# The left key tiles of a unit's two pairs as four 128x64 column tiles in a row

## The chip, the cores and the metric

The kernel runs on one core of one Trainium2 chip. The metric is device microseconds (us) for one execution of the whole program: 609.46 us before the change, the median of three runs (609.01 to 609.54).

Of the core's engines five matter: TensorE (PE; its weight loads are listed as PEld), ScalarE (ACT), VectorE (DVE), GpSimd (POOL) and SyncE (SP), which issues most of the transfers. TensorE writes into PSUM, eight banks of 128 partitions x 512 fp32 values.

## The reference

Attention with normed q and k over 8 batches, 12 heads, 448 tokens and head size 64, and behind it an MLP with a residual over the 768 columns that the heads make together:

```python
q_n, k_n = (rmsnorm(q, g_q), rmsnorm(k, g_k))
scores = 1.0 / np.sqrt(q.shape[-1]) * np.matmul(q_n, k_n.transpose(0, 1, 3, 2))
attn = np.exp(scores - np.max(scores, axis=-1, keepdims=True))
attn = attn / (np.sum(attn, axis=-1, keepdims=True) + 1e-09)
x = np.matmul(attn, v)              # then (batch, 448, 12 * 64)
xn = (x - mu) / np.sqrt(var + 1e-06) * g_ln
out = x + np.maximum(xn @ w_ch1, 0.0) @ w_ch2        # 768 -> 3072 -> 768
```

## The kernel before

**Pairs and units.** Two heads make a pair; a batch has six pairs, so there are 48, numbered through. Pairs are prepared in units (`UNITS`): units 0 and 1 have one pair, units 2 to 24 two. `PAIR_UNIT[p]` gives a pair's unit and its place in it (0 or 1), `UNIT_PAIR[u]` a unit's first pair. From unit 2 on the first pair of a unit is even and the second odd. Units 5 to 24 hold pairs 8 to 47.

**Scores.** A pair's 448 keys per head are six full tiles of 128 keys (three for each head, steps i = 0 to 5) and a rest of 64 keys per head. The two rests form step 6, the left keys. `scores(p, i)` takes a PSUM bank, lets TensorE write 128 keys x 448 queries of scores there, and ScalarE's `Exp` (L357) takes them as fp16 into `E[:, i]`. The contraction is 128 deep: q and k stand as a high and a low fp16 half. The left keys lie in SBUF as 64 columns of head 0, 64 columns of zeros, 64 columns of head 1. Step 6 takes columns 0 to 127 against head 0's queries (L354) and columns 64 to 191 against head 1's (L355), and sums both in one bank: where one writes scores, the other adds zeros. Both stream 448 columns.

**Score banks.** The pool `ps_s` has two banks. After pair 14 (`UNIT_PAIR[DMA_UNIT]`) the bank `tr`, which until then holds transposes, takes every third score, so three banks rotate.

**Values.** `values(p, i)` multiplies `E[:, i]` as weights with v (L389 and L391) into the banks oA and oB; after step 6 `evac_o` divides by the row sums on VectorE. Step 6 of the values takes the left tile of E and `vl`, 130 columns.

**E.** The pool `p_e` has two buffers of seven tiles; pairs alternate between them.

**Order.** Pairs 0 to 6 come in an order written out by hand (`ORDER`). From there `attention()` lists steps, seven a pair: step (p, i) holds pieces of the preparation of coming units, `scores(p, i)`, `values(p - 1, i)`, the statistics for the norm, and, up to pair 13, transposes of the next pair's k (at i = 2) and q (at i = 4) on TensorE with VectorE's copies. From unit 8 on k and q are transposed by DMA from SP (`dma_k`, `dma_q`, L257 to L270). `run_rest` deals these steps out between the chunks of the MLP of the batch before: a chunk is six matmuls of `up` (L631, psH) or `down` (L647, psC). The last 13 chunks of a batch hold no steps, and there the norm of the next batch runs. TensorE, ScalarE, GpSimd and SP take their instructions in the order written; VectorE's order in this part is set by a scheduler. The k and q buffers (`kU`, `qU`) are two each, by unit.

**The flag.** Once, in the last batch, `flag()` sums a check with a matmul of one weight column (L760).

Of the kernel before, what the change touches and what calls it, by code (L numbers as in the profile page):

```python
# [8 lines left out]
FP32 = mybir.dt.float32  # L9
FP16 = mybir.dt.float16  # L10
# [38 lines left out]
EARLY = {5: (42, 49), 6: (47, 56), 7: (61, 69), 8: (75, 83), 9: (89, 97)}  # L49
LN_EXP_SET = 6  # L50
UP_FIRST = 3
REC_LO, REC_HI = 1.0 / 3.0e7, 0.5
K_MAX = 6.0e4
XS = 32.0
# [21 lines left out]
class _Fast:  # L76


    def __init__(self, ctx, tc, sh, q, k, v, gs, g_ln, w1, w2, out):
        self.gs, self.g_ln = gs, g_ln  # L80
        self.tc, self.nc, self.sh = tc, tc.nc, sh
        self.q, self.k, self.v, self.w1, self.w2, self.out = q, k, v, w1, w2, out
        nc = tc.nc
        pool = lambda name, bufs, **kw: ctx.enter_context(tc.tile_pool(name=name, bufs=bufs, **kw))
        self.p_in = pool("p_in", 2)
        self.p_n = pool("p_n", 2)
        self.p_e = pool("p_e", 2)
        self.p_x = pool("p_x", 2)
        self.p_xl = pool("p_xl", 2)
        self.p_m = pool("p_m", 1)  # L90
        self.fix = pool("fix", 1)
        self.ps_tr = pool("ps_tr", 1, space=PSUM)
        self.ps_s = pool("ps_s", 2, space=PSUM)
        self.ps_o = pool("ps_o", 1, space=PSUM)
        self.ps_m = pool("ps_m", 3, space=PSUM)
        fix = self.fix
        self.kU = [fix.tile([128, 1920], FP16, name=f"kU{i}", tag=f"kU{i}") for i in range(2)]
        self.qU = [fix.tile([128, 2, 2, S], FP16, name=f"qU{i}", tag=f"qU{i}") for i in range(2)]
        self.v16 = fix.tile([128, 6, 2, 3, D + 1], FP16, name="v16", tag="v16")
        self.vl = fix.tile([128, 6, 2, D + 1], FP16, name="vl", tag="vl")  # L100
        nc.vector.memset(self.v16[:, :, :, :, D], 1.0)
        nc.vector.memset(self.vl, 0.0)
        nc.vector.memset(self.vl[0:64, :, 0, D], 1.0)
        nc.vector.memset(self.vl[64:128, :, 1, D], 1.0)
        self.rec = fix.tile([128, B * NPAIR, 4, 2], FP32, name="rec_all", tag="rec_all")
        nc.vector.memset(self.rec, 0.01)
        self.rr = fix.tile([128, len(UNITS)], FP32, name="rr_all", tag="rr_all")
        self.rs = fix.tile([128, B, 4], FP32, name="rs_all", tag="rs_all")
        nc.vector.memset(self.rs, RS_LO)
        self.hT = fix.tile([128, NFF, 512], FP16, name="hT", tag="hT")  # L110
        self.tr = self.ps_tr.tile([128, 1024], FP16, name="tr", tag="tr")
        nc.vector.memset(self.tr[:, 64:128].bitcast(FP32), 0.0)
        self.zero_left(DMA_UNIT)
        self.xs, self.xls, self.st = {}, {}, {}
        self.units, self.loads, self.prs = {}, {}, {}
        self.late, self.preps = [], {}

    def zero_left(self, u):

# [218 lines left out]
    def scores(self, p, i):  # L338

        nc = self.nc  # L340
        c = self.prs[p]
        q, left = c["q"], c["left"]
        if i == 0:
            c["E"] = self.p_e.tile([128, 7, S], FP16, tag="E", name="E")
        if p > UNIT_PAIR[DMA_UNIT] and (7 * p + i) % 3 == 2:
            ps = self.ps_tr.tile([128, 512], FP32, tag="tr", name="psS3")
        else:
            ps = self.ps_s.tile([128, 512], FP32, tag="psS", name="psS")
        if i < 6:
            h = i // 3  # L350
            nc.tensor.matmul(ps[:, 0:S], c["main"][:, ts(i, 128)], q[:, ts(h, S)],  # L351
                             start=True, stop=True)
        else:
            nc.tensor.matmul(ps[:, 0:S], left[:, 0:128], q[:, 0:S], start=True, stop=False)  # L354
            nc.tensor.matmul(ps[:, 0:S], left[:, 64:192], q[:, S:2 * S], start=False, stop=True)  # L355
        g = self.group(p, i)
        nc.scalar.activation(out=c["E"][:, i], in_=ps[:, 0:S], func=AFT.Exp,  # L357
                             scale=self.units[PAIR_UNIT[p][0]][3][:, g:g + 1], bias=EXP_BIAS)

        u = PAIR_UNIT[p][0]  # L360
        if i == 6 and UNIT_PAIR[u] == p and u > 4:
            self.least(u)

    def least(self, u):

# [3 lines left out]
    def values(self, p, i):  # L369
        nc = self.nc  # L370
        c = self.prs[p]
        E = c["E"]
        if i == 0:
            if p in (1, 3, 5):
                c["oA"] = self.ps_m.tile([128, 3, 130], FP32, tag="mlp", name="oA")
                c["oB"] = self.ps_m.tile([128, 130], FP32, tag="mlp", name="oB")
            else:
                c["oA"] = self.ps_o.tile([128, 3, 130], FP32, tag="oA", name="oA")
                c["oB"] = self.ps_o.tile([128, 130], FP32, tag="oB", name="oB")
        oA, oB = c["oA"], c["oB"]  # L380
        if i < 6:
            h, j = divmod(i, 3)
            rhs = self.v16[:, p % 6, h, j]
            cs = slice(65 * h, 65 * h + 65)
        else:
            rhs = self.vl[:, p % 6].rearrange("p e d -> p (e d)")
            cs = slice(0, 130)
        for t in range(3):
            nc.tensor.matmul(oA[:, t, cs], E[:, i, ts(t, 128)], rhs,  # L389
                             start=(i == 0 and t == 0), stop=(i == 6 and t == 2))  # L390
        nc.tensor.matmul(oB[:, cs], E[:, i, 320:448], rhs, start=(i == 0), stop=(i == 6))  # L391
        if i == 6:
            self.evac_o(p)

# [73 lines left out]
    def attention(self):  # L468

        n, nu, nb0, done = B * NPAIR, len(UNITS), NPAIR, set(ORDER)  # L470
        todo, last = {}, -9
        for u in range(4, nu):
            p, m = UNIT_PAIR[u], UNITS[u][2]
            st = max(7 * (p - 2 - m) + 2, last + 1, 7 * nb0)
            e = max(7 * (p - 2) - 1, st + 5)
            st, e = EARLY.get(u, (st, e))
            pieces = ["bai", "d", "c", "e", "j", "gv", "k", "l", "m", "w", "x", "y"]
            k = len(pieces) - 2
            if u < DMA_UNIT:
                pieces = pieces[:k]  # L480
            if f"z{u}" in done and u == 4:
                continue
            if u < nu - 2 and f"L{u + 2}" not in done:
                todo.setdefault(e + (8 if u == DMA_UNIT else 1), []).append(
                    lambda u=u: self.load_unit(u + 2))
            last = e
            for x, names in enumerate(pieces):
                at = st + (e - st) * x // (k - 1) if x < k else e + 1 + x - k
                todo.setdefault(at, []).extend(
                    self.prep_ops(u)[y] for y in names  # L490
                    if not {y + str(u), f"z{u}" if y in "vw" else ""} & done)
                if u in (6, 7) and x == 0:
                    todo[at].append(lambda u=u: self.load_w2(u - 6))
        steps, mark = [], [0]

        for p in range(nb0, n + 1):
            for i in range(7):
                c = []
                if i == 0 and p < n and p % NPAIR == 0 and p > nb0:
                    c.append(lambda b=p // NPAIR: self.batch(b))  # L500
                c += todo.pop(7 * p + i, [])
                if p < n and f"S{p}.{i}" not in done:
                    c.append(lambda p=p, i=i: self.scores(p, i))
                if p > nb0:
                    for x in {0: (), 1: (0, 1)}.get(i, (i,)):
                        if f"V{p - 1}.{x}" not in done:
                            c.append(lambda p=p, x=x: self.values(p - 1, x))
                if p > nb0 + 1 and i == 1 and (p - 1) % NPAIR:
                    c.append(lambda p=p: self.stats(p - 2))
                if p + 1 < UNIT_PAIR[DMA_UNIT]:  # L510
                    if i == 2 and f"K{p + 1}" not in done:
                        c.append(lambda p=p: self.trans_k(p + 1))
                    if i == 4 and f"Q{p + 1}" not in done:
                        c.append(lambda p=p: self.trans_q(p + 1))
                if p > nb0 and p % NPAIR == 0 and i == 6:
                    c.append(lambda p=p: self.stats(p - 1))
                if c:
                    steps.append(c)
            if p > nb0 and p % NPAIR == 0:
                mark.append(len(steps))  # L520
        return steps, mark
# [425 lines left out]
```

## Time and profile before

| What | Value |
|---|---|
| median of three runs | 609.46 us |
| span of the profiled execution | 606.9 us |
| that execution's own time | not listed apart; the median is 2.5 us above the span |
| TensorE busy | 579.4 us, 95% |
| TensorE weight loads busy | 346.4 us, 57% |
| ScalarE busy | 359.5 us, 59% |
| VectorE busy | 287.1 us, 47% |
| GpSimd busy | 190.1 us, 31% |
| left scores L354 and L355 | 48 matmuls each, 17.2 and 17.1 us busy |
| exponentials L357 | 336, 635 ns each on average |
| TensorE waiting for an exponential before a full score | 5.3 us, 14 times |
| granted TensorE clock | 0.996 |

A row of the chain or of the timeline gives the start in us from the span's start, the time in us, the engine, the line of the kernel, the operation, what it writes and reads, shapes, and how many were merged; in brackets stands the idle time before it and what ended it. Matmuls are pipelined: a record of a 448-column matmul lasts 0.35 us, but the next starts 0.19 us after it. ScalarE's records overlap in the same way. In the chain each piece has only the time that it adds.

### The profile page before, as it was taken

Reading aid. Unit: us, or ns where it says so; the run is one execution under the profiler, and the core shown is the slowest. Engines: PE = TensorE matmul, PEld = TensorE weight load, DVE = VectorE, ACT = ScalarE, POOL = GpSimd, SP = SyncE. Lnnn points to the kernel's source line nnn. Section 1 sums busy time; section 2 is a strip of 40 time slices with the busy share of each in tenths; the row PEclk is TensorE's granted clock in tenths of the full one; section 3 lists DMA queues with packets and bytes.
Section 4 is the critical chain, followed back from the end, with each engine's and each line's share of the span. In section 5 each row is a group of like instructions: output and inputs, shape, how many; then the busy total and the mean of one; then the engine's idle time right before and its main releaser. Section 6 shows DMA issues by size and latency. Waiting matters only on the chain.

```text
span 606.9 us, 11525 instructions
## 1 busy us (share of the span) xinstructions
PE 579.4 (95%) x4500; PEld 346.4 (57%) x4500; DVE 287.1 (47%) x643; ACT 359.5 (59%) x673; POOL 190.1 (31%) x245
## 2 busy tenths in 40 slices
PE   2887999999999999999999999999999999999995
PEld 1555666655566666655566666655566666654564
DVE  5799567734256256715256255633356322530011
ACT  5996887268743697458753598538754377124200
POOL 3854432233541355332552345423412000000000
PEclk9899999999999999999999999999999999999999
DMA  8999999478954596747955485748733330030011
GB/s 225 275 192 200 214 225 187 103 211 83 149 157 107 89 136 154 174 133 90 126 129 127 114 123 141 188 120 124 125 74 68 92 62 1 31 100 0 1 53 57
DMA packets 130861, 75.29 MB, mean 124 GB/s; under 512 B 96656, under 2 KB 121040, under 8 KB 130800
## 3 DMA queue, kind: packets, MB, share of 16 engines
q1 hardware_dynamic: 114048, 45.12, 38.3%
q0 software_dynamic: 16080, 28.94, 22.1%
q8 instruction: 37, 0.61, 0.5%
q10 hardware_dynamic: 672, 0.43, 0.2%
q14 instruction: 24, 0.20, 0.1%
HBM read 52.36 MB, written 11.01 MB: 104 GB/s over the span
## 4 chain that ended last, share of the span: by engine, by line
PE 90%; DVE 2%; ACT 0%; issue 0%; DVEq 0%
PE psC L647 36%; PE psH L631 35%; PE psS L351 8%; PE oA L389 5%; PE oB L391 2%; PE psS L354 1%; PE psS L355 1%; PE tr L329 0%; PE tr L315 0%; PE psU L677 0%; DVE stat L555 0%; DVE xn L576 0%; DVE x L406 0%; DVE qU L334 0%; ACT E L357 0%
## 5 line engine op out<-in xcount | busy, mean ns | idle before, releaser
L631 PE MATMUL psH<-xnT,w 128*128 128x512 f16 (+1 forms) x1134 | 241.9, 353 | 0.0
L357 ACT ACTIVATE E<-psS,rr_all 128x448 f16<-128x448 f32 x336 | 207.6, 635 | 49.5 <-PE psS L351 44.3
L647 PE MATMUL psC<-w,hT 128*128 128x384 f16 (+1 forms) x1368 | 234.7, 323 | 0.0
L633 ACT ACTIVATE hT<-psH 128x512 f16<-128x512 f32 (+1 forms) x189 | 104.1, 551 | 124.3 <-PE psH L631 122.3
L647 PEld LDWEIGHTS <-hT 128*128 128x128 f16 x1368 | 127.8, 98 | 74.4
L631 PEld LDWEIGHTS <-w 128*128 128x128 f16 x1134 | 102.6, 98 | 80.5
L351 PE MATMUL psS<-qU,kU 128*128 128x448 f16 x288 | 100.9, 358 | 8.0 <-ACT E L357 5.3
L389 PEld LDWEIGHTS <-E 128*128 128x128 f16 x1008 | 71.2, 99 | 48.7 <-issue 4.1
L228 POOL TENSOR_TENSOR qkv<-qkv,gprod 128x896 f32<-128x896 f32 x21 | 43.7, 2080 | 95.3 <-issue 49.5
L389 PE MATMUL oA<-v,E 128*128 128x65 f16 x864 | 67.0, 194 | 0.1
L651 DVE SCALAR_TENSOR_TENSOR x<-psC,rs_all,x 128x384 f32<-128x384 f32 x48 | 28.9, 615 | 72.0 <-PE psC L647 71.5
L404 DVE RECIPROCAL rec_all<-oA 128x6 f32<-128x6 f32 x48 | 9.3, 193 | 94.0 <-PE oA L389 93.8
L391 PE MATMUL oB<-v,E 128*128 128x65 f16 x288 | 52.0, 194 | 0.1
L127 POOL DMA_DIRECT2D qkv<-in_k_dram x14 | 11.2, 799 | 129.8 <-ACT E L357 60.3
L217 DVE TENSOR_REDUCE ssq<-khl 128x14 f32<-128x896 f32 (+1 forms) x24 | 25.6, 1065 | 44.6 <-ACT khl L214 44.5
L351 PEld LDWEIGHTS <-kU 128*128 128x128 f16 x288 | 28.2, 99 | 25.8 <-issue 6.1
L217 DVE TENSOR_REDUCE ssq<-qn 128x14 f32<-128x896 f32 (+1 forms) x25 | 26.1, 1046 | 21.9 <-ACT qn L214 21.8
L67 DVE SCALAR_TENSOR_TENSOR qn<-qkv,rr_all 128x256 f16<-128x256 f32 (+1 forms) x72 | 26.3, 424 | 15.3 <-ACT rr_all L221 15.3
L391 PEld LDWEIGHTS <-E 128*128 128x128 f16 x336 | 32.7, 97 | 0.3 <-DVE xl L411 0.2
L239 DVE TENSOR_TENSOR khl<-qkv,khl 128x896 f16<-128x896 f32 x21 | 22.7, 1083 | 10.6 <-ACT khl L236 9.7
L406 DVE TENSOR_TENSOR x<-oA,rec_all 128x384 f32<-128x384 f32 x48 | 26.8, 558 | 1.5
L555 DVE BATCH_NORM_STATS2 stat<-x 128x6 f32<-128x256 f32 (+1 forms) x75 | 26.2, 404 | 0.6
(104 smaller groups left out, 448.4 us busy)
## 6 DMA issues: line engine op xcount, KB each, us to landing
out_dram<-x SPq DMA_DIRECT2D x20, 384.0 KB, 2.5
qkv<-in_k_dram POOLq DMA_DIRECT2D x14, 384.0 KB, 3.9
qkv<-in_q_dram POOLq DMA_DIRECT2D x14, 384.0 KB, 5.2
qkv<-in_v_dram POOLq DMA_DIRECT2D x14, 384.0 KB, 7.8
w<-in_moe_w_ch_dram POOLq DMA_DIRECT2D x3, 1536.0 KB, 12.6
w<-in_moe_w_ch_dram POOLq DMA_DIRECT2D x2, 2304.0 KB, 24.1
qkv<-in_k_dram SPq DMA_DIRECT2D x7, 384.0 KB, 6.6
qkv<-in_q_dram SPq DMA_DIRECT2D x7, 384.0 KB, 6.1
```

Source lines behind the costliest of these rows:

```text
L67: nc.vector.scalar_tensor_tensor(out=out, in0=x, scalar=8.0, in1=r.unsqueeze(2).broadcast_to([x.shape[0], g, D]), op0=ALU.mult, op1=ALU.mult)
L217: nc.vector.tensor_reduce(out=c["ssq"][:, n], in_=c["sq", n], axis=AX.X, op=ALU.add)
L228: (nc.vector if u in DVE_KG else nc.gpsimd).tensor_tensor(out=c["t"][1], in0=c["t"][1], in1=sh.gprod.unsqueeze(1).broadcast_to([128, g, D] ...
L351: nc.tensor.matmul(ps[:, 0:S], c["main"][:, ts(i, 128)], q[:, ts(h, S)], start=True, stop=True)
L357: nc.scalar.activation(out=c["E"][:, i], in_=ps[:, 0:S], func=AFT.Exp, scale=self.units[PAIR_UNIT[p][0]][3][:, g:g + 1], bias=EXP_BIAS)
L389: nc.tensor.matmul(oA[:, t, cs], E[:, i, ts(t, 128)], rhs, start=(i == 0 and t == 0), stop=(i == 6 and t == 2))
L391: nc.tensor.matmul(oB[:, cs], E[:, i, 320:448], rhs, start=(i == 0), stop=(i == 6))
L406: nc.vector.tensor_tensor(out=x[:, :, 128 * hp:128 * hp + 128].rearrange("p t (e d) -> p t e d", e=2), in0=oA[:, :, :, 0:D], in1=rec[:, 0: ...
L631: nc.tensor.matmul(ps[:, 0:N], sh.w1[:, dc, ts(f, 128)], xnT[:, dc, 0:N], start=(dc == 0), stop=(dc == NDC - 1))
L633: nc.scalar.activation(out=hT[:, f, 0:N], in_=ps[:, 0:N], func=AFT.Relu)
L647: nc.tensor.matmul(ps[:, 0:g[1]], hT[:, f, ts(t, 128)], sh.w2[:, f, cols], start=(f == 0), stop=(f == NFF - 1))
L651: nc.vector.scalar_tensor_tensor(out=x[:, cols], in0=ps[:, 0:g[1]], scalar=self.rs[:, b, t:t + 1], in1=x[:, cols], op0=ALU.mult, op1=ALU.add)
```

## The change

For units 5 to 24 the left keys of both pairs of a unit are scored together, in step 6 of the even pair. Two score banks are taken. For each pair, head 0's 64 left keys are loaded as 64 weight columns and their scores written to partitions 0 to 63, head 1's to partitions 64 to 127 of the same bank, without the columns of zeros and without summing. So there are four matmuls in a row with 128 x 64 weights, and two exponentials behind them. In step 6 of the odd pair no score is left.

- Step 6 of the scores stands behind step 6 of the values now, in all pairs that `attention()` lists.
- An odd pair's left exponentials go to a tile of their own, `EL`, as its `E` isn't there yet; `E` has seven tiles for even pairs and six for odd ones, each kind with one buffer.
- The bank of a score is chosen by a running count of scores (`n_scores`), no longer by 7p + i.

The full tiles, the left keys of pairs 0 to 7, the MLP and the transfers stay as they are.

```diff
+TWO_LEFT = 5
-        self.p_e = pool("p_e", 2)
+        self.p_e = pool("p_e", 1)
...
     def scores(self, p, i):
-        q, left = c["q"], c["left"]
+        u, w = PAIR_UNIT[p]
+        both = u >= TWO_LEFT and i == 6
         if i == 0:
-            c["E"] = self.p_e.tile([128, 7, S], FP16, tag="E", name="E")
-        if p > UNIT_PAIR[DMA_UNIT] and (7 * p + i) % 3 == 2:
-            ps = self.ps_tr.tile([128, 512], FP32, tag="tr", name="psS3")
-        else:
-            ps = self.ps_s.tile([128, 512], FP32, tag="psS", name="psS")
+            k = 7 - p % 2
+            c["E"] = self.p_e.tile([128, k, S], FP16, tag=f"E{k}", name="E")
+        if both and w:
+            return
+        ps = [self.score_bank(p + d) for d in range(2 if both else 1)]
...
+        elif both:
+            for d, x in enumerate(ps):
+                cd = self.prs[p + d]
+                for e in range(2):
+                    nc.tensor.matmul(x[64 * e:64 * e + 64, 0:S], cd["left"][:, 128 * e:128 * e + 64],
+                                     cd["q"][:, ts(e, S)], start=True, stop=True)
...
+        for d, x in enumerate(ps):
+            if i < 6 or (p + d) % 2 == 0:
+                o = c["E"][:, i]
+            else:
+                o = self.prs[p + d]["EL"] = self.p_e.tile([128, S], FP16, tag="EL", name="EL")
+            g = self.group(p + d, i)
+            nc.scalar.activation(out=o, in_=x[:, 0:S], func=AFT.Exp,
+                                 scale=self.units[u][3][:, g:g + 1], bias=EXP_BIAS)
...
+    def score_bank(self, p):
+        self.n_scores += 1
+        if p > UNIT_PAIR[DMA_UNIT] and self.n_scores % 3 == 2:
+            return self.ps_tr.tile([128, 512], FP32, tag="tr", name="psS3")
+        return self.ps_s.tile([128, 512], FP32, tag="psS", name="psS")
...
     def values(self, p, i):
-        E = c["E"]
+        E = c["EL"] if i == 6 and p % 2 else c["E"][:, i]
...
-                if p < n and f"S{p}.{i}" not in done:
+                if p < n and f"S{p}.{i}" not in done and i < 6:
                     c.append(lambda p=p, i=i: self.scores(p, i))
                 if p > nb0:
                     for x in {0: (), 1: (0, 1)}.get(i, (i,)):
                         if f"V{p - 1}.{x}" not in done:
                             c.append(lambda p=p, x=x: self.values(p - 1, x))
+                if p < n and i == 6 and f"S{p}.6" not in done:
+                    c.append(lambda p=p: self.scores(p, 6))
```

More of the change, by code (lines that the diff above doesn't have):

```diff
@@ L115, in __init__ @@
         self.units, self.loads, self.prs = {}, {}, {}
-        self.late, self.preps = [], {}
+        self.late, self.preps, self.n_scores = [], {}, 0
     def zero_left(self, u):
@@ L349, in scores @@
+        if both and w:
+            return
+        ps = [self.score_bank(p + d) for d in range(2 if both else 1)]
         if i < 6:
             h = i // 3
-            nc.tensor.matmul(ps[:, 0:S], c["main"][:, ts(i, 128)], q[:, ts(h, S)],
+            nc.tensor.matmul(ps[0][:, 0:S], c["main"][:, ts(i, 128)], c["q"][:, ts(h, S)],
                              start=True, stop=True)
-        else:
-            nc.tensor.matmul(ps[:, 0:S], left[:, 0:128], q[:, 0:S], start=True, stop=False)
-            nc.tensor.matmul(ps[:, 0:S], left[:, 64:192], q[:, S:2 * S], start=False, stop=True)
@@ L356, in scores @@
[L356 to L360, printed above, removed]
+        elif both:
[4 more added lines that the diff above has]
+                                     cd["q"][:, ts(e, S)], start=True, stop=True)
+        else:
+            left, q = c["left"], c["q"]
+            nc.tensor.matmul(ps[0][:, 0:S], left[:, 0:128], q[:, 0:S], start=True, stop=False)
+            nc.tensor.matmul(ps[0][:, 0:S], left[:, 64:192], q[:, S:2 * S], start=False, stop=True)
@@ L388, in values @@
         for t in range(3):
-            nc.tensor.matmul(oA[:, t, cs], E[:, i, ts(t, 128)], rhs,
+            nc.tensor.matmul(oA[:, t, cs], E[:, ts(t, 128)], rhs,
                              start=(i == 0 and t == 0), stop=(i == 6 and t == 2))
-        nc.tensor.matmul(oB[:, cs], E[:, i, 320:448], rhs, start=(i == 0), stop=(i == 6))
+        nc.tensor.matmul(oB[:, cs], E[:, 320:448], rhs, start=(i == 0), stop=(i == 6))
         if i == 6:
```

## The prediction

> **What bounds the kernel now.** I read the page's busy times first, then the chain that ended last (by engine, then in order of time), then TensorE's timeline around the only small weight tile the kernel has, then ScalarE's timeline where the left scores stand.
>
> ```profile
> span 606.9 us, 11525 instructions
> PE 579.4 (95%) x4500; PEld 346.4 (57%) x4500; DVE 287.1 (47%) x643; ACT 359.5 (59%) x673; POOL 190.1 (31%) x245
> ...
> PE 90%; DVE 2%; ACT 0%; issue 0%; DVEq 0%
> ```
>
> TensorE (PE) is busy 95% of the span and is 90% of the chain; no other engine is near. The span is 606.9 us and the median of the three runs 609.46, so about 2.5 us lie around the span; which run was profiled is not listed, and I take that offset as fixed.
>
> ```profile
> 302.90 0.97 PE psC L647 x6
> 303.87 0.19 PE psS L354
> 304.06 0.19 PE psS L355
> 304.25 0.17 PE oA L389 x3
> 304.42 0.06 PE oB L391
> 304.48 1.95 PE psC L647 x12
> ```
>
> This is one step of a pair that ends with left keys. The pieces touch: 302.90 + 0.97 = 303.87, and so on. The two left scores (L354, L355) cost 0.19 us of TensorE each, 0.378 a pair, with no idle time, and whatever TensorE is spared there shortens the kernel unless a new wait takes it back.
>
> **What the left scores cost after.** The change touches 20 units, 40 pairs. Before, a unit's two pairs stream 4 x 448 columns through a full-width array, 4 x 0.189 = 0.756 us. After, there are four matmuls whose weights fill 64 of 128 columns, low, high, low, high. If a low and a high tile stream side by side, the unit takes 2 x 0.189 = 0.378 us; if one after the other, 0.756 as before. No row shows two matmuls side by side, so these are the two ends. I take the lower one: the two tiles use disjoint columns of the array and write disjoint partitions of one PSUM bank, and the nearest row, the weight loads (346.4 us busy beside a gapless TensorE), shows that loading and streaming already run together. It is a judgement, and its chance is given below.
>
> Entering and leaving that form has a price that one place in the trace shows: the one-column matmul of the flag (L760), the only one whose weights do not fill the array.
>
> ```profile
> 541.41 0.59 PE L631 MATMUL psH<-xnT,w 128*128 128x512 f16 x2
> 541.94 0.19 PE L760 MATMUL psF<-cnt,ones 128*1 128x1 f32 x2
> 542.06 0.61 PE L631 MATMUL psH<-xnT,w 128*128 128x512 f16 x2
> ...
> 541.93 0.09 PEld L760 LDWEIGHTS psF<-cnt,ones 128*1 128x1 f32 x2 [0.42 <-issue]
> 542.05 0.11 PEld L631 LDWEIGHTS <-w 128*128 128x128 f16 x2
> ```
>
> Matmuls of 512 columns follow each other by 0.216 us, so the stream of the two at 541.41 ends at 541.84; L760 starts at 541.94, 0.09 us late, and its weight load waits with it (elsewhere loads are issued a whole matmul ahead). The two one-column matmuls stand 0.03 apart, and the next 512-column one starts at 542.06, some 0.09 after the second; its pair takes 0.61 instead of 0.59, a bare weight load of about 0.01 to 0.02. So: 0.09 in, 0.09 + 0.01 out. (The rows are fp32 and one column wide; that the same holds for 64 fp16 columns is assumed.) The Trainium skill, TensorEngine Tiling (Array Packing), section Key Properties, says that a change of the tiling mode drains the TensorE. By that rule the drain is paid twice a unit, and the trace agrees with 0.09 us at each border.
>
> Between the borders the first tile's load is bare and the high tile starts a load later. I put 0.027 us for the two together (twice the bare 128-column load above); the lower end is 0, the upper 2 x 0.098, the whole duration of a load record. Unit after: 0.09 + 0.027 + 0.378 + 0.10 = 0.595, with 0.02 for four issues about 0.615. Gain 0.756 - 0.615 = 0.14 a unit, x 20 = 2.8 us (ends: 3.6 with free loads; -0.6, a loss, with 0.098 bare before each low-high pair).
>
> **New waits for ScalarE (ACT).** Two score banks are now wanted at once, and two exponentials (0.63 us a record, 0.52 from start to start) follow each other, so a bank comes free later than before. Pairs 8 to 14 rotate two banks, later pairs three. With two, the second pair's tiles wait for the exponential of score 5, the next pair's score 0 for the first left exponential; with three, the next pair's score 1 does. What matters is how late that exponential is.
>
> ```profile
> 76.10 0.63 ACT L357 ACTIVATE E<-psS,rr_all 128x448 f16<-128x448 f32 x1
> ...
> 76.99 0.97 ACT L214 ACTIVATE qn<-qkv 128x896 f32<-128x896 f32 x1
> 77.83 0.65 ACT L357 ACTIVATE E<-psS,rr_all 128x448 f16<-128x448 f32 x1
> ...
> 76.14 0.35 PE L354 MATMUL psS<-qU,kU 128*128 128x448 f16 x1
> ...
> 77.72 0.35 PE L351 MATMUL psS<-qU,kU 128*128 128x448 f16 x1
> ```
>
> Pair 8: ScalarE squares first, and the left exponential ends at 78.48. After the change TensorE does the value matmuls of that step first (0.22), enters (0.09), scores; the second pair's tiles would start 0.53 after 76.14 but the exponential of score 5 ends at 76.73, 0.59 after: wait 0.1. Score 0 of pair 9 would then come at 76.14 + 0.96 + 0.97 = 78.07 and its bank is free at 78.5: wait 0.45. In the same manner pair 10 (exponential of score 5 ends 0.71 after its left score, left exponential 2.08 after): 0.23 + 0.08; pair 12: 0.23, then a long run of L647 matmuls covers the rest. In the stages with three banks two places are tight:
>
> ```profile
> 233.05 1.02 ACT L236 ACTIVATE khl<-qkv 128x896 f16<-128x896 f32 x1
> 233.89 1.23 ACT L357 ACTIVATE E<-psS,rr_all 128x448 f16<-128x448 f32 x2
> ...
> 233.87 0.54 PE L351 MATMUL psS<-qU,kU 128*128 128x448 f16 x2
> ```
>
> Pair 22 (left score at 232.29): the left exponential ends at 234.59, and scores 0 and 1 of pair 23 stand together; score 1 would come at 232.29 + 0.85 + 0.97 + 0.19 = 234.30 and now needs that bank: wait 0.34. Pair 34, at 371.18, is the same. At the other pairs the bank is free before it is wanted (pair 20: free 2.86 after, wanted 2.98; pairs 16, 18, 24, 26, 44 by 0.5 us or more). Sum 0.55 + 0.31 + 0.23 + 0.68 = 1.8; gaps of 0.12 and 0.07 that TensorE has today at 79 to 81 us go, as its scores come later: about 1.6 us. Behind a waiting score TensorE holds an MLP chunk and value matmuls; ScalarE's relu and VectorE's evacuation, which wait for those, come later by as much, and both have idle time (59% and 47% busy), so nothing else becomes late. Ends: 0.6 (only pairs 8 and 10's larger waits) and 2.6 (pairs 20 and 32 too, 0.5 more).
>
> **Moves that I cost at nothing.** The odd pair's left scores come seven steps earlier. For units 5 to 7 they need VectorE's copies of k and q two steps earlier; for pair 9 the q copy ends at 75.68, before 76.14, and the others end before their scores too. For later units the DMA transposes on SP land units ahead; the one into the left keys' columns was held by the odd pair's left score (issue at 207.80, score at 207.33) and is now held only by the queue, whose transpose before it lasted until 207.71, so nothing comes earlier. The order of SP and GpSimd is unchanged. VectorE's order shifts: the subtraction L239 at 186.95 goes behind the evacuations and norms, to some 194; the transpose that reads it is issued at 206.43, after waiting for the buffer, so 12 us cover it, and without that cover it would be 1 us a batch. Single E buffers change no reuse distance: even and odd pairs alternated between two already, and the separate odd tile is written just after its last reader in TensorE's order.
>
> **Sum.** 609.46 - 2.8 + 1.6 = 608.3 us.
>
> **The rivals.**
> - *The tiles stream one after the other.* For: no row shows overlap. Against: nothing in the rows but the disjoint columns. Then a unit costs 0.756 + 0.24 instead of 0.756: + 0.24 x 20 = 4.8, with the waits 1.6 (less, as everything is later: 1.2): 615.4, slower. It decides from the point where a low-high pair takes over 0.22 us instead of 0.19: (0.756 - 0.237 - 0.08) / 2, where 20 x 0.08 are the waits.
> - *Overlap in part: the loads of the 64-column tiles are not hidden.* For: around L760 the load was not issued ahead. With 0.098 bare before each low-high pair the unit costs 0.09 + 0.196 + 0.378 + 0.10 + 0.02 = 0.78, 0.5 us lost in all, and the waits remain: 611.5; with half of that, 610. The Trainium skill, TensorE: Matmul & The Clock Gate, section Measured speedup vs the span model, reports 2.38 times for three column tiles instead of 3; an estimate by that share would make a pair 0.24 us, the unit 0.72, and the time 610.2. The same page's span model (a few ns a tile) would leave the sum as it is, and no run here shows either.
> - *The waits don't come.* If ScalarE, spared the odd step's exponential, is less late at pairs 8, 10, 22 and 34, the 2.8 stands nearly whole: 606.7. Against: at those places it was late through squares and copies of the same step, which do not move.
>
> **How the numbers follow.** Forecast 0.62 (own range 606.6 to 609.9), waits absent 0.08, part overlap 0.13, one after the other 0.17. Within 0.2% (1.2 us, about what a measurement of this kernel can tell from no change) is 608.2 to 610.7. The forecast lies near the border: 0.36 of its 0.62 below it, 0.25 within, 0.01 above. Part overlap: 0.05 within, 0.08 above. Faster 0.36 + 0.08 = 0.44, same 0.30, slower 0.01 + 0.08 + 0.17 = 0.26. The range 606.2 to 612.5 leaves out the serial case and a little below, under 0.2.
>
> **What the profile after would show.** Right: the starts of a low and a high tile some 0.03 us apart, 0.19 to the next low one; 0.09 before the first and after the last; waits of TensorE for the exponentials at pairs 8, 10, 22 and 34, 1.6 us more in all. Wrong: starts 0.19 apart throughout (serial), or loads that stand bare between the tiles; or TensorE idle at other units' left scores. The prediction fails most easily by the overlap.

## The result, and the profile after

The changed kernel takes 607.37 us (median of 16 runs, 606.53 to 608.26) against 609.04 us (608.23 to 609.71) for the kernel before in the same number of runs. The ratio is 0.9974, with a 95% interval of 0.9967 to 0.9980: 0.26% faster, 1.6 us. The forecast was 608.3 us, 1.2 us less than before.

The lines of the page that answer to those shown of before (busy times, chain by engine):

```profile
span 604.8 us, 11485 instructions
PE 575.8 (95%) x4500; PEld 340.3 (56%) x4500; DVE 287.3 (48%) x643; ACT 358.4 (59%) x673; POOL 184.0 (30%) x245
...
PE 88%; ACT 2%; DVE 2%; issue 0%; DVEq 0%
```

TensorE still bounds the kernel, but the chain now passes through ScalarE too, 2% of it: at the new waits it runs back through the exponentials and what ScalarE did ahead of them. The span is 2.1 us shorter. Of this, 0.6 lies ahead of the first MLP matmul (at 52.58 us before, at 51.95 after), where the granted clock of the first 60 us was 0.97 in the one profile and 1.00 in the other; over all runs of this study it lies between 51.95 and 53.91, so it is not the change's. From that matmul to the last one TensorE took 547.86 us before and 546.22 after, 1.64 less, close to the 1.67 between the medians. I use this stretch for all runs below and call it TensorE's stretch. It comes from one execution of each kernel, and for the runs below it lies up to 0.9 us off what the ratios of the medians give.

One unit's left scores after, in TensorE's timeline (start, length, what, how many merged), and its weight loads:

```profile
302.68 0.33 PE L408 MATMUL oA<-vl,EL 128*128 128x130 f16 x3
302.85 0.22 PE L410 MATMUL oB<-vl,EL 128*128 128x130 f16 x1
303.00 0.57 PE L359 MATMUL psS<-qU,kU 128*64 128x448 f16 x4
303.50 0.66 PE L668 MATMUL psC<-w,hT 128*128 128x384 f16 x3
...
303.00 0.14 PEld L359 LDWEIGHTS <-kU 128*64 128x64 f16 x4
303.50 0.11 PEld L668 LDWEIGHTS <-hT 128*128 128x128 f16 x2 [0.36 <-issue]
```

Four matmuls of 448 columns begin at 303.00 and the next full-width one at 303.50; four full-width ones took 0.756. The single records behind this merged line start as follows (ns from the first; the last two columns are the full-width matmul behind the row and what it is late itself):

```
              low   high   low   high  | next start  + late
unit at 303.00  0      3    213   216  |   501          13
the row before it: the last value matmul's stream ends 96 before the first start
```

So a high tile starts 3 to 4 ns behind its low one, and the second low one 0.213 after the first: a stream of 0.187 (448 columns) and 0.026 more. I take the 0.026 for the bare load in front of the first pair, since the records of the first two tiles last 0.377 and those of the second two 0.352. With 0.096 to enter, 0.098 to leave behind the last stream and 0.013 for the next bare load the row costs 0.611 us. Seventeen of the twenty rows cost 0.610 or 0.611.

The waits for ScalarE at pair 8 and at pair 22, TensorE's timeline:

```profile
75.83 0.70 PE L359 MATMUL psS<-qU,kU 128*64 128x448 f16 x4
76.46 1.15 PE L652 MATMUL psH<-xnT,w 128*128 128x384 f16 x6
77.89 0.35 PE L353 MATMUL psS<-qU,kU 128*128 128x448 f16 x1 [0.28 <-ACT E L371]
...
232.28 1.15 PE L668 MATMUL psC<-w,hT 128*128 128x384 f16 x6
233.26 0.35 PE L353 MATMUL psS<-qU,kU 128*128 128x448 f16 x1
233.80 0.35 PE L353 MATMUL psS<-qU,kU 128*128 128x448 f16 x1 [0.19 <-ACT E L371]
```

At pair 8 the row is longer (0.70 instead of 0.57: its second low tile waits 0.11 for the bank), and score 0 of pair 9 starts at 77.89 where the matmuls ahead of it end their stream at 77.45: 0.45 lost (the bracket counts from the end of the pipelined record, so it shows less). At pair 22 score 1 starts 0.54 behind score 0 instead of 0.19: 0.35 lost. ScalarE's side at pair 22:

```profile
231.84 0.55 ACT L654 ACTIVATE hT<-psH 128x384 f16<-128x384 f32 x1
232.21 1.02 ACT L237 ACTIVATE khl<-qkv 128x896 f16<-128x896 f32 x1
233.05 0.70 ACT L371 ACTIVATE E<-psS,rr_all 128x448 f16<-128x448 f32 x1
233.56 0.71 ACT L371 ACTIVATE EL<-psS,rr_all 128x448 f16<-128x448 f32 x1
```

The row starts at 231.78; ScalarE has a relu and a copy to do first, and the first left exponential ends at 233.75, just ahead of 233.80.

**Where the time went.** Left scores before: 20 x 0.756 = 15.12 us. The rows after, summed with what waits for the second bank inside them (pairs 8, 10, 12): 12.85. Waits of the next pair's scores that are new: 0.45 + 0.07 + 0.35 + 0.35 = 1.22. Gaps of TensorE over 0.04 us that are gone (at 79, 81, 99, 234 and 373 us of the profile before): 0.46. Sum: -15.12 + 12.85 + 1.22 - 0.46 = -1.51, against -1.64 in TensorE's stretch; the other 0.13 stays open.

### The profile page after: what moved, and what is told of

It reads as the page before. It is cut to its first block, busy times and chain, and to the rows that moved or that the text cites. A ratio compares the mean times of both kernels' runs of the same rounds, so it can differ in the third digit from the quotient of the medians.

```text
span 604.8 us, 11485 instructions
## 1 busy us (share of the span) xinstructions
PE 575.8 (95%) x4500; PEld 340.3 (56%) x4500; DVE 287.3 (48%) x643; ACT 358.4 (59%) x673; POOL 184.0 (30%) x245
## 4 chain that ended last, share of the span: by engine, by line
PE 88%; ACT 2%; DVE 2%; issue 0%; DVEq 0%
PE psC L668 36%; PE psH L652 35%; PE psS L353 8%; PE oA L408 5%; PE oB L410 2%; PE psS L359 1%; ACT E L371 1%; PE tr L316 0%; ACT khl L215 0%; PE psU L698 0%; DVE stat L576 0%; ACT hT L654 0%; PE tr L330 0%; DVE xn L597 0%; DVE x L425 0%
## 5 line engine op out<-in xcount | busy, mean ns | idle before, releaser
L371 ACT ACTIVATE E<-psS,rr_all 128x448 f16<-128x448 f32 x312 | 193.4, 635 | 48.7 <-PE psS L353 47.8
L408 PEld LDWEIGHTS <-E 128*128 128x128 f16 x936 | 64.5, 98 | 44.5 <-issue 5.1
L410 PEld LDWEIGHTS <-E 128*128 128x128 f16 x312 | 30.2, 97 | 0.2 <-DVE xl L430 0.2
```

The source lines that it names most:

```text
L371: nc.scalar.activation(out=o, in_=x[:, 0:S], func=AFT.Exp, scale=self.units[u][3][:, g:g + 1], bias=EXP_BIAS)
L408: nc.tensor.matmul(oA[:, t, cs], E[:, ts(t, 128)], rhs, start=(i == 0 and t == 0), stop=(i == 6 and t == 2))
L410: nc.tensor.matmul(oB[:, cs], E[:, 320:448], rhs, start=(i == 0), stop=(i == 6))
```

## The experiments

Two theories stand against each other. Mine: a low and a high tile stream side by side at the ordinary rate, each border of a row costs about 0.1 us, and part of the gain goes to waits because ScalarE comes late to two exponentials. Rivals: 64 weight columns stream faster one after the other; the borders cost nothing and the loads are what is paid; the move itself helps or hurts. Each ratio is to runs of the kernel before on the same chip.

### Low, low, high, high

```diff
-            for d, x in enumerate(ps):
-                cd = self.prs[p + d]
-                for e in range(2):
+            for e in range(2):
+                for d, x in enumerate(ps):
+                    cd = self.prs[p + d]
```

> Same four tiles a unit, but in the order low, low, high, high instead of low, high, low, high. Theory (a low and a high tile stream side by side, two low ones can't): the row takes three streams of 0.187 us instead of two, 0.80 us a unit instead of 0.61; 20 x 0.187 = 3.7 us more than the changed kernel, so about 2 us slower than the kernel before. Rival (64 weight columns stream faster, or what is saved is the summing): the order doesn't matter, time as the changed kernel, 1.6 us faster than before.

Measured 608.15 us, ratio 0.9982 (0.9969 to 0.9995). The 3.7 us did not come: a row with no wait costs 0.614 us instead of 0.611, and TensorE's stretch is 0.88 longer than the changed kernel's.

```profile
304.11 0.57 PE L359 MATMUL psS<-qU,kU 128*64 128x448 f16 x4
304.61 0.66 PE L668 MATMUL psC<-w,hT 128*128 128x384 f16 x3
...
76.06 0.89 PE L359 MATMUL psS<-qU,kU 128*64 128x448 f16 x4
```

The single records tell why. In the row at 304.11 the four start at 0, 8, 214 and 220 ns. The first and the third carry the waits for a free bank, which only low tiles have; the second and the fourth carry the signals that the program gives to high ones. So the first high tile started 8 ns behind the first low one, ahead of the second low one that stands before it in the program. At pair 8, where the second low tile had to wait for its bank, the starts are 0, 323, 326 and 540: the first high tile, behind the waiting one, was held with it and ran 3 ns after it. These rows fit one reading: instructions are let go in order, wait by wait, and after that each half of the array takes its own next one. At pairs 8 and 10, where the second low tile waits, the row costs one stream of 0.187 more than in the changed kernel: 0.93 instead of 0.75 us, and 1.05 instead of 0.86. At pair 12 it costs 1.60 instead of 0.87, for another reason: ScalarE's square ahead of the exponential of score 5 starts at 108.75 here and at 107.54 in the changed kernel, and the second low tile waits for that exponential. Why the square is later I did not follow.

```profile
109.29 0.38 PE L359 MATMUL psS<-qU,kU 128*64 128x448 f16 x1
110.28 0.57 PE L359 MATMUL psS<-qU,kU 128*64 128x448 f16 x3 [0.61 <-ACT E L371]
...
108.75 0.95 ACT L215 ACTIVATE khl<-qkv 128x896 f32<-128x896 f32 x1 [0.75 <-DMA kU<-khl]
109.61 0.62 ACT L371 ACTIVATE E<-psS,rr_all 128x448 f16<-128x448 f32 x1
```

These three rows make 1.1 us, and the scores behind the rows of pairs 8 and 10 wait 0.26 less; together that is 0.85 of the 0.88. My theory's number was wrong, because it had the two halves share one order. But the run doesn't decide for the rival either, which also said that the order does not matter. The next two do.

### One tile twice, both tiles twice

```diff
-                for e in range(2):
+                for e in (0, 1, 0):          # the second kernel: (0, 1, 0, 1)
```

> Each pair's low tile is scored a second time behind the high one (low, high, low; the same scores once more). Theory (low and high tiles stream side by side at the full-width rate, two low ones one after the other): one more stream of 0.187 us a pair, 40 x 0.187 = 7.5 us more than the changed kernel, about 5.9 slower than before. Rival (tiles run one after the other, but 64 columns at twice the rate): 40 x 0.094 = 3.7 us more, about 2.1 slower than before.

> Both tiles of each pair are scored a second time (low, high, low, high). Theory: the second high tile rides beside the second low one, so no more than with the low one twice: 7.5 us more than the changed kernel, about 5.9 slower than before. Rival (one after the other at twice the rate): twice what the low one alone costs, 7.5 against 3.7. So the theory says that both of these runs take the same time, the rival that this one takes 3.7 us more.

Measured 613.08 us and 612.62 us, ratios 1.0062 (1.0042 to 1.0083) and 1.0062 (1.0042 to 1.0082). The same row in each, first with six matmuls, then with eight:

```profile
307.07 0.94 PE L359 MATMUL psS<-qU,kU 128*64 128x448 f16 x6
307.95 0.66 PE L668 MATMUL psC<-w,hT 128*128 128x384 f16 x3
```

```profile
305.74 0.95 PE L359 MATMUL psS<-qU,kU 128*64 128x448 f16 x8
306.62 0.66 PE L668 MATMUL psC<-w,hT 128*128 128x384 f16 x3
```

Both rows hold TensorE for 0.88 us: the two further high tiles cost 3 ns. Against the changed kernel's 0.50 it is 0.38 more, two streams of 0.187. The eight single records of the second row start at 0, 3, 213, 216, 402, 405, 591 and 595 ns: two by two, and the later pairs 0.19 apart, which leaves no room for an overlap in part either. That is the side-by-side theory; at double rate the second row would have taken 0.19 longer than the first. The total rose by less than the 7.5 us forecast for both (by the ratios 3.8 over the kernel before and 5.4 over the changed one; 5.9 and 6.1 over the changed one in TensorE's stretch). With longer rows ScalarE has time: the waits at pairs 22 and 34 are gone, that at pair 8 fell from 0.45 to 0.21, and the waits for the second bank, which stand inside the rows, nearly vanish in their further streams (the rows grew by 6.9 and 7.1 us, not 7.5). The Trainium skill, TensorE: Matmul & The Clock Gate, section Measured speedup vs the span model, gives a few ns a tile for tiles side by side; the 3 to 4 ns here agree.

### The row cut in two

```diff
             for d, x in enumerate(ps):
+                if d:
+                    between()            # the step's four value matmuls
...
-                    c.append(lambda p=p: self.scores(p, 6))
+                    c.append(lambda p=p: self.scores(p, 6, lambda: self.values(p - 1, 6)))
```

> The row is cut in two by the step's four value matmuls with full-width weights: low, high, values, low, high. Theory (each border of a row costs about 0.1 us, entering and leaving alike, and a bare load of 0.025): one more round trip, 0.235 us a unit, 4.7 us in all, less 0.5 as the second bank is then free in pairs 8 to 12: 4.2 us more than the changed kernel, 2.5 us slower than before. Rival (what is paid at the borders is the wait for the bank or the load alone): 20 x 0.025, 0.5 us more than the changed kernel.

Measured 612.32 us, ratio 1.0044 (1.0031 to 1.0057).

```profile
304.80 0.38 PE L361 MATMUL psS<-qU,kU 128*64 128x448 f16 x2
305.11 0.34 PE L413 MATMUL oA<-vl,EL 128*128 128x130 f16 x3
305.29 0.22 PE L415 MATMUL oB<-vl,EL 128*128 128x130 f16 x1
305.44 0.38 PE L361 MATMUL psS<-qU,kU 128*64 128x448 f16 x2
```

Each half row without a wait costs 0.421 us: 0.096 in, 0.003, 0.309 to the next full-width start (0.024 load, 0.187 stream, 0.098 out), 0.013. Twice 0.421 is 0.231 more than 0.611, as expected from the border price (0.235). Rows summed: 16.91 us against 12.85, 4.1 more; the waits at pairs 22 and 34 fell from 0.35 to 0.12, and TensorE's stretch is 3.4 longer than the changed kernel's (4.3 by the ratios, 4.2 expected). The Trainium skill, TensorEngine Tiling (Array Packing), section Key Properties, says that changing the tiling mode drains the array; the trace agrees, with 0.096 us at each entry (0.125 at the two that also wait for a bank) and 0.098 at each exit.

### The move alone

```diff
-                for e in range(2):
-                    nc.tensor.matmul(x[64 * e:64 * e + 64, 0:S], cd["left"][:, 128 * e:128 * e + 64], ...
+                left, q = cd["left"], cd["q"]
+                nc.tensor.matmul(x[:, 0:S], left[:, 0:128], q[:, 0:S], start=True, stop=False)
+                nc.tensor.matmul(x[:, 0:S], left[:, 64:192], q[:, S:2 * S], start=False, stop=True)
```

> All of the change but the small tiles: both pairs' left keys together, own tile for the odd exponentials, but full-width weights with zeros and sums as before. Theory (the gain is the tiles', the waits are the move's): streaming as before, new waits for exponentials of 1.2 us (pairs 8, 10, 12, 22, 34), old gaps of 0.45 gone: 0.7 us slower than before, 2.3 slower than the changed kernel. Rival (the move itself helps): faster than before.

Measured 610.57 us, ratio 1.0014 (1.0001 to 1.0026), 0.66 us more in TensorE's stretch, against 0.7 expected. Pair 22, with four full-width scores 0.19 apart, and scores 0 and 1 of pair 23:

```profile
234.26 0.35 PE L359 MATMUL psS<-qU,kU 128*128 128x448 f16 x1
...
234.83 0.35 PE L360 MATMUL psS<-qU,kU 128*128 128x448 f16 x1
235.02 1.14 PE L668 MATMUL psC<-w,hT 128*128 128x384 f16 x6
235.99 0.74 PE L353 MATMUL psS<-qU,kU 128*128 128x448 f16 x2
```

The two scores take 0.74 us, where two that touch take 0.54. So the waits are there without the small tiles: 0.40 at pair 8, 0.20 at pairs 22 and 34, 0.16 at pairs 10 and 12 for the second bank. The move costs, and the tiles gain.

### A row for each pair

```diff
-        if both and w:
-            return
-        ps = [self.score_bank(p + d) for d in range(2 if both else 1)]
+        ps = [self.score_bank(p)]
...
-            for d, x in enumerate(ps):
-                cd = self.prs[p + d]
...
+            cd, x = c, ps[0]
```

> The small tiles without the pairing: each pair scores its own left keys in its own step, low and high in a row, one bank at a time. Theory: entering 0.096, bare load 0.025, stream 0.187, leaving 0.098 + 0.013, issue 0.004 make 0.42 us a pair against 0.378 with full width: 40 x 0.045 = 1.8 us slower than before, no new waits. Rival (borders cheaper when a row is short, since the drain hides under the load): 40 x 0.1 = 4 us faster than before at best.

Measured 610.21 us, ratio 1.0012 (1.0002 to 1.0021): 0.7 us slower than before, not 1.8. The rows cost what was expected, 0.421 us each against 0.378, 1.7 us in all:

```profile
304.42 0.38 PE L356 MATMUL psS<-qU,kU 128*64 128x448 f16 x2
304.73 0.66 PE L665 MATMUL psC<-w,hT 128*128 128x384 f16 x3
```

But 0.74 us of gaps went that I had left in: six places (at 234, 243, 373, 382 and twice at 520 us before) where values waited for VectorE to empty oA and oB. Step 6 of the values stands ahead of the left scores in this kernel and VectorE gets 0.42 us more. The last 0.3 us between 1.7 - 0.74 and 0.7 is only in part accounted for (two other gaps are 0.08 shorter). Small tiles pay here only when two pairs share a row: one round trip for both.

### The exponentials first

```diff
+                two = i == 6 and p < n and PAIR_UNIT[p][0] >= TWO_LEFT and PAIR_UNIT[p][1] == 0
-                c += todo.pop(7 * p + i, [])
+                prep = todo.pop(7 * p + i, [])
+                if not two:
+                    c += prep
...
                     c.append(lambda p=p: self.scores(p, 6))
+                if two:
+                    c += prep
```

> The changed kernel, but in the even pairs' step 6 the pieces of preparation (squares, copies on ScalarE) stand behind the left scores and their two exponentials instead of ahead. Theory (TensorE waits at pairs 8, 10, 22 and 34 because ScalarE does a square or a copy of about 0.85 to 1 us first): the waits of 0.45, 0.07, 0.35 and 0.35 go, those of 0.11, 0.23 and 0.23 for the second bank stay: 1.2 us less than the changed kernel, 2.9 less than before. Rival (two exponentials in a row are too slow whatever stands ahead, or the late pieces delay something else): same as the changed kernel or slower.

Measured 607.50 us, ratio 0.9968 (0.9956 to 0.9980). In TensorE's stretch it is 0.85 us shorter than the changed kernel, not 1.2; the intervals of the two ratios overlap, so the times alone don't tell them apart. The waits at pairs 8, 10, 22 and 34 are gone, as expected. But with two banks a new one came at pair 9, here with ScalarE's row under TensorE's:

```profile
80.97 0.20 PE L410 MATMUL oB<-v,E 128*128 128x65 f16 x1
81.28 0.35 PE L353 MATMUL psS<-qU,kU 128*128 128x448 f16 x1
...
79.34 0.98 ACT L215 ACTIVATE qn<-qkv 128x896 f32<-128x896 f32 x1
80.18 0.52 ACT L659 ACTIVATE hT<-psH 128x384 f16<-128x384 f32 x1
80.55 0.68 ACT L371 ACTIVATE E<-psS,rr_all 128x448 f16<-128x448 f32 x1
```

The square that stood ahead of the left exponentials now stands ahead of pair 9's first one, which ends at 81.23; score 2 of pair 9 wants that bank and starts at 81.28, 0.29 late, and score 3 is 0.08 late (in the kernel before, 0.12 and 0.07 were lost at these two scores). The delay was pushed on, and with two banks part of it met TensorE again two scores later.

### Small tiles from unit 8 on

```diff
-TWO_LEFT = 5
+TWO_LEFT = 8
```

> The changed kernel with the small tiles from unit 8 on alone; units 5 to 7, which have two score banks, keep the old form, and the order of ScalarE's pieces stays as changed. Theory: 17 units x 0.146 = 2.5 us, waits of 0.35 at pairs 22 and 34 stay, those of pairs 8 to 12 (0.57 for the second bank, 0.52 for the first) are not made, old gaps of 0.3 stay: 0.4 us less than the changed kernel, 2.0 less than before, and 0.6 more than the run with the exponentials first from unit 8. Rival (the two-bank units' waits are made good later): 0.4 us more than the changed kernel.

> As the run with the exponentials first, but units 5 to 7 (two score banks) keep the old form. Theory: 17 units x 0.145 = 2.5 us, no new waits, old gaps of 0.3 us stay: 2.6 us less than before, within 0.3 us of the run with all 20 units, since those three units gain 0.44 and pay 0.57 of waits for the second bank. Rival (the two-bank units still gain): over 0.5 us slower than the run with all 20.

The first kernel has this edit alone, the second has it with the exponentials first. Measured 607.17 us, ratio 0.9968 (0.9956 to 0.9980), and 606.87 us, ratio 0.9957 (0.9944 to 0.9971); 2.04 and 2.73 us less than before in TensorE's stretch. The second has the lowest ratio of the study: 17 rows of 0.61, no wait at pairs 22 and 34 (the scores 0 and 1 of pair 23 touch again), and all else as before:

```profile
231.87 0.57 PE L359 MATMUL psS<-qU,kU 128*64 128x448 f16 x4
232.37 1.15 PE L673 MATMUL psC<-w,hT 128*128 128x384 f16 x6
233.36 0.54 PE L353 MATMUL psS<-qU,kU 128*128 128x448 f16 x2
...
232.30 0.71 ACT L371 ACTIVATE E<-psS,rr_all 128x448 f16<-128x448 f32 x1
232.82 0.71 ACT L371 ACTIVATE EL<-psS,rr_all 128x448 f16<-128x448 f32 x1
233.34 1.03 ACT L237 ACTIVATE khl<-qkv 128x896 f16<-128x896 f32 x1
```

Of the expectations, 2.0 and 2.6 us less than before came out. The three units with two banks gain 0.44 us in the changed kernel and pay 1.16 in waits (their rows are 0.64 longer, the next scores 0.52 late), 0.84 when the 0.32 of gaps that went there is set against it: 0.40 lost, and without them the first kernel's stretch is 0.39 shorter. The intervals of the second kernel and of the changed one just overlap (0.9944 to 0.9971 and 0.9967 to 0.9980), so that it is faster than the changed kernel rests on the traces: 1.1 us in TensorE's stretch.

## Why the prediction was right

- **The side-by-side streams** were a judgement with no row behind it, and the whole gain hung on it; that it came true was not read out of the trace of before. They are shown now: six and eight tiles take the same time. By this the serial rival falls, and the one of overlap in part.
- **The row's cost.** Forecast 0.615 us, measured 0.611. The borders, read off the flag's one-column fp32 matmul as 0.09 in and 0.10 out, are 0.096 and 0.111 for 64 fp16 columns. The bare load was put at 0.027 and is 0.024 to 0.026, paid once for both tiles, since they load side by side too: the starts that were to be 0.03 apart are 0.003 to 0.004 apart. The second pair's loads are hidden while the first pair streams, so the rival of bare loads fell. That the sum met so well was partly luck: the 0.02 for four issues had no row, 0.003 of it is seen, and the rest happens to stand in for borders that are 0.017 dearer than forecast. One end was also added up wrongly: with free loads the prediction's own terms give 20 x (0.756 - 0.588) = 3.4 us, not 3.6.
- **The waits.** Forecast at pairs 8, 10, 12, 22 and 34: 0.55, 0.31, 0.23, 0.34, 0.34. Measured 0.56, 0.30, 0.23, 0.35, 0.35, and no others over 0.04 us. Reading when ScalarE ends its exponential in the old trace, and when TensorE would want the bank, was enough, because ScalarE's own order ahead of those places did not move. The rival without these waits fell.
- **The gaps that go.** Here a term was mis-sized: 0.19 us put down, 0.46 measured. Missed were two of 0.07 at 234 and 373 us, where values waited for VectorE's evacuation, which now starts earlier as the values' last step comes ahead of the row (and the values behind it come later through the new wait), and one of 0.12 at 99 us ahead of q's transposes, whose cause stays open.
- **The moves costed at nothing** show nothing: no gap at a unit's first score, and none at the batch borders beyond those of before.

Sum by the measured terms: 2.9 for the tiles (20 x 0.145), 1.8 for waits, 0.46 for gaps, 1.5 to 1.6 us in all, where 1.2 was forecast. The forecast of 608.3 stands 0.9 over the measured median, 0.4 of it because the kernel before itself had 609.04 in the longer series and not 609.46. What came, 0.26% faster, is just beyond the 0.2% that the prediction calls the same. The chance of "faster", 0.44, was the highest of the three; it was held low by the forecast's nearness to that border (0.25) and by the rivals of serial and of partial overlap (0.17 and 0.13), which nothing in the trace of before could exclude.

## What to carry to other kernels

Where TensorE bounds a kernel and weights fill only half of its columns, two such tiles can stream in the time of one (shown here for 128 x 64 fp16 weights and 448 columns), but a row of them pays a fixed price at its two borders (0.21 us here, more than one stream of 448 columns), so tiles have to be collected until a row saves more than that: one pair a row lost 0.04 us, two pairs gained 0.145. Collecting asks for more result banks at once; look up in the trace when the engine that empties them is late, and order its work so that the emptying comes first. Where the banks are too few, much of the delay only moves: with two banks, 0.52 us of waits at pairs 8 and 10 came back as 0.36 at pair 9.

## What the runs showed of the hardware that I had not expected

Matmuls of different column halves can pass each other. In the program order low, low, high, high the first high tile began 8 ns behind the first low one, and the second low one 214 ns behind it; a row cost 0.614 us instead of the 0.80 that one common order would give. The run with the low tile twice shows it too: the second pair's high tile starts at 217 ns, beside the first pair's second low tile, and its own low tile, ahead of it in the program, at 402. A semaphore wait in between does hold back what stands behind it: where the second low tile could start only 0.32 us after the first, the first high tile began 3 ns after it. The Trainium skill, TensorE: Matmul & The Clock Gate, section The mechanism, has matmuls start and end strictly in program order; these rows differ from it for tiles in different column halves, and the measurement decides. It would follow that the last matmul in the program need not be the last one to finish where tiles are mixed; no run here has a row that shows that, and whether the kernels' signals rely on the order was not tried.
